# Three constant products instead of one on TensorE between the steps on wo's two halves

## The chip, the cores and the metric

The kernel runs on one core of a Trainium2 chip (trn2). The metric is the device time of one execution in microseconds; of several executions the median is given. Engine names are those of the profile: PE is TensorE, PEld its weight loads, DVE VectorE, ACT ScalarE, POOL GpSimd, SP SyncE; a q behind a name means the engine's sequencer or its DMA issues.

## The reference

One decode step for two batch rows, a gated mix of attention over the last 4096 cached positions and a dense layer with Mish:

```
B, Sq, D = 2, 1, 512;  Hq, Hkv, Sk, Dh = 32, 8, 32768, 128;  F = 1792
W = min(4096, max(256, Sk // 4))
def _A_ref(x, k_cache, v_cache, wq, wo):
    q = (x @ wq).reshape(B, Sq, Hq, Dh).transpose(0, 2, 1, 3)
    k, v = the last W positions of k_cache, v_cache, each head repeated Hq // Hkv times
    p = softmax(einsum("bhqd,bhkd->bhqk", q, k) * Dh ** -0.5)
    return einsum("bhqk,bhkd->bhqd", p, v).reshape(B, Sq, Hq * Dh) @ wo
def _B_ref(x, w1, b1, w2):
    h = x @ w1 + b1
    return (h * tanh(softplus(h))) @ w2
g = sigmoid((x * gate_w).sum(-1, keepdims=True))
return g * _A_ref(...) + (1 - g) * _B_ref(...)
```

All arrays are float32. What has to be read is about 91 MB: the eight heads' K and V (4 MB each), wq and wo (8 MB each), w1 and w2 (3.5 MB each).

## The kernel before

**Chunks and steps.** The big arrays come in as chunks of 128 partitions x 8192 float32 (4 MB) that are loaded in turn into two buffers, `buf_b` and `buf_a` (`load`, L349 to L359). A chunk is sixteen slots of 512 columns. A *step* on a buffer (`slots`, L369) multiplies each slot with 32 weight columns on TensorE; the product of slot s goes to rows 32·(s mod 4) to 32·(s mod 4)+31 of one PSUM bank, so that four slots in a row use four different column strips of the array. The eleven steps on `buf_b` are wq's first half, K of heads 0 to 7, w1 and wo's second half; the eleven on `buf_a` are wq's second half, V of heads 0 to 7, wo's first half and the larger part of w2. Between them stand "turns" (L409 to L417): four transposes of `turn` into `t_b`, a small product with `ones`, and one *constant product*.

**The constant product** (`idle_work`, L392) multiplies the 128x128 identity by four copies of itself into the bank `b_idle`, which nothing reads. It has no data to wait for and is there to occupy TensorE.

**The loop.** TensorE's program is a loop of three bodies, and a register `n` counts the steps on `buf_a`: it starts at `FULL - steps_a` = 6 (L399) and is raised by one behind each step on `buf_a` (L420). After each step L421 sets `spin` to `n & 16`, that is 0 up to V of head 7 and 16 after wo's first half. As long as `n` is at most 16, L422 goes to the body "spin" (L402): one constant product, `spin` raised by one (L404), and back to the constant product while `spin` is under `SPINS` = 5 (L405). So there are five constant products behind each of the steps before wo, and one behind the step on wo's first half, where `spin` is 17 after one pass. Then "step_b" runs on `buf_b`, which at that point is wo's second half; with `n` = 16 it goes on to "step_a" without a turn (L408), and that step is w2's.

**The end of the program**, in order, with the numbers that the prediction follows:

- step on wo's first half (`buf_a`, bank `g_a`). When it is done, SP issues the five last loads (L363 to L366): w2's blocks 0 to 7 and 8 to 10 into slots 5 to 12 and 13 to 15 of `buf_a` (semaphores `s4`, `s12`), and three single blocks into `rest` (`sr`). ACT copies `g_a` into `sums` (L316), and POOL sets up the weights of w2's step in `la` (L317, L318);
- the constant product (L393 in the body "spin");
- step on wo's second half (`buf_b`, bank `g_b`), which waits at slot 0 for the landing of its chunk (`sb`);
- step on w2 (`buf_a`, bank `g_a`): it waits at slot 0 for `la` (`sa`), at slot 5 for `s4`, at slot 13 for `s12` (L419; the waits are L372). Slots 0 to 4 have zero weights and wait for no transfer;
- "products" (L423, `finish`, L334): the first two blocks in `rest`, each behind its landing, then `sums` times a fold matrix, then the last block in `rest`, all four into `b_fin`. `sums` becomes ready by two additions on DVE: `g_b` when wo's second half is done (L321) and `g_a` when the step on w2 is done (L322);
- DVE copies `b_fin` into `res` (L344) and SP stores it (L367).

Loads go out from SP in program order, each into its buffer as soon as the step that used the buffer before is done.

## Time and profile before

| | us |
|---|---|
| median of 3 runs (219.75 to 219.83) | 219.81 |
| the profiled execution's own time | 219.8 |
| its span, first to last instruction | 217.8 |
| PE busy / DVE / ACT / POOL | 158.2 / 26.8 / 16.6 / 14.2 |
| constant products (61, each two records of 128x512) | 58.3 |
| read from HBM, mean rate | 91.24 MB, 419 GB/s |
| mean granted TensorE clock | 0.961 |

The page gives the busy time of each engine and a picture of the span in 40 slices; a PEclk digit under 9 there is a slice in which TensorE's clock was granted only in part. The view of windows gives, for chosen stretches of the span, each engine's busy time, the granted clock and the rate of the DMAs. The timeline lists instructions in order, merged, with the idle time before them in brackets. Each float32 product on TensorE leaves two matmul records.

### The profile page before, as it was taken

What the parts mean: (1) busy time and instruction counts of PE and PEld (TensorE: products, weight loads), DVE (VectorE), ACT (ScalarE), POOL (GpSimd) and SP (SyncE); (2) the same over time, 40 slices, a digit from 0 to 9 for tenths busy, and PEclk for the clock granted to TensorE, in tenths of its full rate; (3) what the DMA queues carried; (4) which work ended last, traced back from release to release, by engine and by line L of the source; (5) the groups of instructions that cost most, each with busy time, mean ns of one, the idle gap of its engine ahead of it and who ended that gap; (6) DMA issues with size and microseconds to landing.
All of it is one profiled execution on the core that took longest, in us unless ns stands there. A gap on an engine that the chain in (4) does not pass through costs nothing. (4 is left out here: it accounts for less than half of the span.)

```text
span 217.8 us, 2358 instructions
## 1 busy us (share of the span) xinstructions
PE 158.2 (73%) x948; PEld 58.0 (27%) x948; DVE 26.8 (12%) x49; ACT 16.6 (8%) x39; POOL 14.2 (7%) x44
## 2 busy tenths in 40 slices
PE   0048976897577649965983976599399689989495
PEld 0012222332122223322321322132123233343132
DVE  0000001030102102110310301030103103062011
ACT  0021001200200110020002002000200120020100
POOL 4040101000100100010010001000100030003000
PEclk9999999999999988997999999799969999999979
DMA  8999999999999999999999999999999999999992
GB/s 290 392 476 391 475 391 475 391 475 391 475 391 475 391 475 391 475 391 475 391 469 397 469 397 469 397 469 391 469 397 469 397 445 421 469 397 463 391 407 97
DMA packets 3985, 91.30 MB, mean 419 GB/s; under 512 B 576, under 2 KB 656, under 8 KB 1168
## 3 DMA queue, kind: packets, MB, share of 16 engines
q1 hardware_dynamic: 3840, 91.27, 97.6%
q10 hardware_dynamic: 144, 0.01, 0.1%
q8 instruction: 1, 0.02, 0.0%
HBM read 91.24 MB, written 0.04 MB: 419 GB/s over the span
## 5 line engine op out<-in xcount | busy, mean ns | idle before, releaser
L373 PE MATMUL bank<-buf_b,zeros 128*32 128x512 f32 x352 | 44.3, 648 | 23.7 <-PEq L372 23.7
L373 PE MATMUL bank<-buf_a,zeros 128*32 128x512 f32 x352 | 46.1, 671 | 17.9 <-PEq L372 17.9
L393 PE MATMUL bank<-ident 128*128 128x512 f32 x122 | 58.3, 608 | 0.0
L393 PEld LDWEIGHTS bank<-ident 128*128 128x128 f32 x122 | 21.2, 190 | 25.6 <-issue 25.6
L373 PEld LDWEIGHTS bank<-buf_b,zeros 128*32 128x32 f32 x352 | 12.9, 117 | 53.2 <-issue 53.2
L373 PEld LDWEIGHTS bank<-buf_a,zeros 128*32 128x32 f32 x352 | 13.8, 121 | 49.2 <-issue 49.2
L412 PE MATMUL bank<-ident,turn 128*128 128x128 f32 x60 | 9.4, 280 | 15.6 <-PEq L410 15.6
L209 ACT ACTIVATE turn<-bank,mx 128x512 f32<-128x512 f32 x8 | 5.5, 687 | 132.5 <-DVE mx L207 132.5
L230 DVE TENSOR_TENSOR om<-bank,pick 128x512 f32<-128x512 f32 x8 | 5.5, 692 | 73.6 <-PE bank L373 73.6
L412 PEld LDWEIGHTS bank<-ident,turn 128*128 128x128 f32 x60 | 6.3, 140 | 28.3 <-issue 28.3
L207 DVE TENSOR_REDUCE mx<-bank 128x1 f32<-128x512 f32 x8 | 5.5, 692 | 63.5 <-PE bank L373 63.5
L202 POOL COPY zeros<-zeros 128x512 f32<-128x512 f32 x8 | 4.9, 616 | 125.7 <-PE bank L373 125.7
L233 DVE TENSOR_REDUCE od<-om 128x128 f32<-128x512 f32 x8 | 8.3, 1036 | 0.3
L211 ACT COPY zeros<-bank 128x512 f32<-128x512 f32 x8 | 4.7, 586 | 7.9 <-PE bank L413 7.9
L413 PE MATMUL bank<-zeros,ones 128*128 128x66 f32 x30 | 5.0, 249 | 0.0
L413 PEld LDWEIGHTS bank<-zeros,ones 128*128 128x128 f32 x30 | 4.5, 191 | 0.0
L182 ACT ACT_TABLE_LOAD x1 | 1.3, 1283 | 14.6 <-POOL ident L165 14.6
L158 POOL MEMSET zeros<- 128x2490 f32 x1 | 2.2, 2173 | 0.3 <-POOLq L478 0.3
L226 POOL TENSOR_TENSOR ms<-ms,top 8x64 f32<-8x64 f32 x2 | 0.6, 309 | 23.9 <-DVE top L224 23.8
L321 DVE TENSOR_TENSOR sums<-sums,bank 128x512 f32<-128x512 f32 x1 | 0.7, 687 | 11.5 <-PE bank L373 11.5
L175 DVE TENSOR_REDUCE zeros<-xg 128x2 f32<-128x8 f32 x1 | 0.2, 163 | 13.9 <-POOL xg L162 13.9
L273 ACT COPY turn<-od 128x512 f32<-128x512 f32 x1 | 0.6, 617 | 14.6 <-PE bank L413 14.6
(68 smaller groups left out, 22.6 us busy)
## 6 DMA issues: line engine op xcount, KB each, us to landing
buf_b<-in_k SPq DMA_DIRECT2D x8, 4096.0 KB, 15.5
buf_a<-in_v SPq DMA_DIRECT2D x8, 4096.0 KB, 14.9
buf_b<-in_wq SPq DMA_DIRECT2D x1, 4096.0 KB, 12.3
buf_a<-in_wq SPq DMA_DIRECT2D x1, 4096.0 KB, 21.5
buf_a<-in_wo SPq DMA_DIRECT2D x1, 4096.0 KB, 14.4
buf_b<-in_wo SPq DMA_DIRECT2D x1, 4096.0 KB, 15.5
buf_b<-in_w SPq DMA_DIRECT2D x1, 3584.0 KB, 14.3
buf_a<-in_w SPq DMA_DIRECT2D x1, 2048.0 KB, 8.8
```

The lines of the kernel that those rows point to most:

```text
L158: zero_ok = t = pool.add(lambda: G.memset(zeros, 0.0))
L182: act.add(lambda: S.activation(turn, g_b, AF.Copy, scale=SCALE), xs_ok, id_ok, at("B q0"), sem=st)
L202: pool.add(lambda kv=kv: G.tensor_copy(lb.rearrange("p (m j q) -> p m j q", m=BN, j=NJ), qz[:, kv, : BN * Q].rearrange("p (m q) -> p m q", ...
L207: mx_ok = dve.add(lambda kv=kv: V.tensor_reduce(mx[:, kv : kv + 1], g_b, axis=AX.X, op=ALU.max, negate=True), before_b)
L209: act.add(lambda kv=kv: S.activation(turn, g_b, AF.Exp, bias=mx[:, kv : kv + 1], accum_out=ls[:, kv : kv + 1]), mx_ok, sem=st)
L211: act.add(lambda: S.copy(la, t_b), at(f"T p{kv}"), sem=sa, by=1 if kv else 2)
L230: t = dve.add(lambda: V.tensor_tensor(om, g_a.rearrange("p (m d) -> p m d", m=BN), pick[:, :, None].to_broadcast([P, BN, DH]), op=ALU.mult ...
L233: dve.add(lambda kv=kv: V.tensor_reduce(od[:, kv], om.rearrange("p m d -> p d m"), axis=AX.X, op=ALU.add), t, sem=sa)
L373: ins = T.matmul(bank[Q * (s % NJ) : Q * (s % NJ) + Q, :], weights[:, s * Q : (s + 1) * Q], buf[:, s * D : (s + 1) * D], start=(s < NJ), s ...
L393: T.matmul(b_idle, ident, ident[:, None, :].to_broadcast([P, NT, P]), start=True, stop=True)
L412: T.transpose(t_b[:, c * P : (c + 1) * P], turn[:, c * P : (c + 1) * P], ident)
L413: T.matmul(b_s[:, : HKV * BH + B], ones, kx, start=True, stop=True).then_inc(pe.sem, 1)
```

## The change

The loop counter of the constant products goes up in strides of eight to a limit of 40:

```diff
-SPINS = 5
+SPINS = 40
 FULL = 16
+STRIDE = 8
...
             part("spin")
             idle_work()
-            eng.reg_add(spin, spin, 1)
+            eng.reg_add(spin, spin, STRIDE)
             eng.br_lt(spin, SPINS, "spin", "step_b")
```

From `spin` = 0 the counter passes 8, 16, 24, 32, 40: five constant products, as before. From `spin` = 16, behind the step on wo's first half, it passes 24, 32, 40: three constant products instead of one. No other engine's program changes, and the list of TensorE's instructions stays the same; only the number of passes through one loop differs. All lines of the kernel from the new constant on stand one line lower.

## The prediction

> **What bounds the kernel now.** I read the picture of the span first. The rows are PE's busy tenths, the granted clock, the DMA share and the rate, in 40 slices of 5.44 us:

> ```profile
> PE   0048976897577649965983976599399689989495
> PEclk9999999999999988997999999799969999999979
> DMA  8999999999999999999999999999999999999992
> GB/s 290 392 476 391 475 391 475 391 475 391 475 391 475 391 475 391 475 391 475 391 469 397 469 397 469 397 469 391 469 397 469 397 445 421 469 397 463 391 407 97
> ```

> The transfers fill the span up to the last slice, so a change on TensorE counts only where TensorE is late against the transfers, and that is the end. Six digits of PEclk stand under 9. At the first five of them (slices 15, 16, 19, 26 and 30) the transfers run on regardless; the last, the 7 in the last slice but one, lies just ahead of the end. The chain of work that ended last says the same (start, length, what):

> ```profile
> 205.49 0.04 issue
> 205.54 8.80 PE bank L373 x64
> ...
> 214.43 0.70 DVE sums L322
> 215.13 0.04 issue
> 215.18 0.69 PE bank L334 x16
> ...
> 215.89 0.29 DVE res L344
> ```

> From 205.54 us on nothing but TensorE's two last steps and a short tail sets the end. The timeline of PE there (start, length, line, operands, records, idle before), with one earlier run of five constant products:

> ```profile
> 181.26 4.56 PE L393 MATMUL bank<-ident 128*128 128x512 f32 x10
> ...
> 197.85 3.64 PE L373 MATMUL bank<-buf_a,zeros 128*32 128x512 f32 x32 [0.45 <-PEq L372]
> 201.42 1.13 PE L393 MATMUL bank<-ident 128*128 128x512 f32 x2
> 205.54 5.34 PE L373 MATMUL bank<-buf_b,zeros 128*32 128x512 f32 x32 [2.99 <-PEq L372]
> 210.66 3.64 PE L373 MATMUL bank<-buf_a,zeros 128*32 128x512 f32 x32
> 214.10 0.65 PE L334 MATMUL bank<-rest,zeros 128*32 128x128 f32 x16
> 215.18 0.43 PE L334 MATMUL bank<-sums,zeros 128*32 128x128 f32 x8 [0.43 <-DVE sums L322]
> 215.42 0.40 PE L334 MATMUL bank<-rest,zeros 128*32 128x128 f32 x8
> ```

> Two steps with the same 32 records stand side by side: the one on w2 goes from 210.66 to 214.10, 3.44 us; the one on wo's second half goes from 205.54 to 210.66, 5.12 us, 1.68 us more. Ahead of the slow one lie the single constant product and 2.99 us of idle.

> **Why that step is slow.** The view of windows, cut into stretches of 3.41 us whose edges I laid on the point where records turn slow (206.58). Columns: stretch, its length, busy us of PE, PEld, DVE, ACT, POOL with counts, granted clock, DMA share, GB/s:

> ```profile
> 97.35:100.76 3.41, 0.80 (x9) 0.28 (x12) 0.00 (x0) 0.00 (x0) 0.00 (x0) 1.00 0.94 404
> 100.76:104.18 3.42, 3.42 (x24) 1.09 (x20) 0.00 (x0) 0.00 (x0) 0.00 (x0) 0.50 0.93 402
> ...
> 117.83:121.24 3.41, 1.60 (x16) 0.65 (x20) 0.00 (x0) 0.00 (x0) 0.00 (x0) 1.00 0.89 384
> 121.24:124.66 3.42, 3.42 (x24) 1.21 (x17) 1.29 (x2) 0.00 (x0) 0.00 (x0) 1.00 1.00 431
> ...
> 134.90:138.31 3.41, 1.45 (x8) 0.62 (x6) 0.00 (x0) 0.59 (x1) 0.00 (x0) 1.00 0.91 394
> 138.31:141.72 3.41, 2.75 (x16) 0.92 (x20) 0.00 (x0) 0.00 (x0) 0.00 (x0) 0.50 0.94 404
> ...
> 199.75:203.16 3.41, 2.80 (x21) 0.61 (x10) 0.00 (x0) 0.59 (x1) 0.72 (x4) 1.00 1.04 452
> 203.16:206.58 3.42, 1.04 (x12) 0.50 (x16) 0.00 (x0) 0.00 (x0) 0.00 (x0) 1.00 0.94 402
> 206.58:209.99 3.41, 3.41 (x23) 1.08 (x16) 0.00 (x0) 0.00 (x0) 0.00 (x0) 0.50 0.97 412
> 209.99:213.40 3.41, 3.41 (x36) 1.26 (x32) 0.69 (x1) 0.00 (x0) 0.00 (x0) 1.00 1.00 399
> ```

> Read each row's PE busy together with the clock of the next row. After 0.80, 1.45 and 1.04 us of work the next stretch has half the clock; after 1.60 and 2.80 us it has all of it; a busy stretch at half clock brings the full one back. So on this grid the clock is halved for 3.41 us when the stretch before was busy for less than something between 1.45 us (42%) and 1.60 us (47%). The cost here is half of 3.41, 1.71 us, against the 1.68 us by which the step is too long: one halved stretch explains it.

> [...]

> **The change part by part.** It adds two passes of one loop at one place. All other loops keep their counts: from 0 the counter reaches 40 after five passes, from 16 after three.

> *The two products.* Five take 4.56 us and one takes 1.13, so one more is (4.56 - 1.13) / 4 = 0.86 us, and three take 1.13 + 1.72 = 2.85 us: they end at 201.42 + 2.85 = 204.27 instead of 202.55. The next step starts at 205.54, so 1.27 us of idle are left and the added 1.72 us cost nothing as long as wo's second half lands no earlier than now. That start is set by a landing, as the rows of the waits in the steps (L372; each row is one wait, "first and last start" is its time) and of the loads show:

> ```profile
> L372 PEldq EVENT_SEMAPHORE  x1: 51/51/51, 205.4 to 205.4; - x1
> L372 PEldq EVENT_SEMAPHORE  x1: 51/51/51, 210.3 to 210.3; - x1
> L372 PEldq EVENT_SEMAPHORE  x1: 51/51/51, 212.2 to 212.2; - x1
> buf_b<-in_wo SPq DMA_DIRECT2D x1, 4096.0 KB, 15.5
> buf_a<-in_w SPq DMA_DIRECT2D x1, 2048.0 KB, 8.8
> buf_a<-in_w SPq DMA_DIRECT2D x1, 768.0 KB, 10.3
> rest<-in_w SPq DMA_DIRECT2D x1, 256.0 KB, 10.7
> ...
> 189.91 0.33 SPq L350 DMA_DIRECT2D buf_b<-in_wo  x1
> 201.54 0.80 SPq L350 DMA_DIRECT2D buf_a<-in_w  x2
> 202.39 1.38 SPq L350 DMA_DIRECT2D rest<-in_w  x3
> ```

> wo's second half lands at 189.91 + 15.5 = 205.4, where its wait ends; the first product follows 0.1 us later. Nothing else is queued behind the two products but that step: `b_idle` has no reader, and SP, ACT and POOL are released by the step before.

> *The clock.* In the stretch from 203.16 to 206.58 PE now works 204.27 - 203.16 = 1.11 us longer, 2.15 us in all (63%), above the 1.60 us after which the clock stayed. So 206.58 to 209.99 keeps the full clock, and the step on wo's second half takes 3.44 us: 205.54 to 208.98, 1.68 us earlier than before.

> *What is late next.* Not all of the 1.68 us reaches the end, for the step on w2 waits at slot 5 and slot 13 for its own transfers. The first one lands at 201.54 + 8.8 = 210.34, the second, issued at about 201.9, at 201.9 + 10.3 = 212.2, just where the wait rows above stand; before, TensorE's sequencer had run ahead to these waits and the array was later than both. Now the array is ahead. Its pace at full clock shows in the weight loads of that step, four column strips at a time:

> ```profile
> 210.66 0.16 PEld L373 LDWEIGHTS bank<-buf_a,zeros 128*32 128x32 f32 x4 [0.27 <-issue]
> 211.09 0.16 PEld L373 LDWEIGHTS bank<-buf_a,zeros 128*32 128x32 f32 x4 [0.27 <-issue]
> ```

> Four records, one of each of four slots, per 0.43 us, two such groups per four slots: 0.86 us. Slots 0 to 3 run from 208.98 to 209.84; slot 4 follows alone; slots 5 to 7 start at 210.34 + 0.1 = 210.44 (the 0.1 as between 205.4 and 205.54) and end at 211.30; slots 8 to 11 end at 212.16; slots 13 to 15 start at 212.2 + 0.1 = 212.3 and end at 213.16. Before, the step ended at 214.10, so it ends 0.94 us earlier.

> *The tail.* The addition on DVE (214.43 before, 0.33 behind the step's end) starts at 213.49, takes its 0.70, and 0.05 later, at 214.24 instead of 215.18, the fold product follows; the last product runs at 214.48 instead of 215.42. The last block lands 10.7 us after its issue, the third of the row at 202.39 with 1.38 us for three, so at about 203.3 + 10.7 = 214.0, and 0.1 later its product could run: 214.1, in time for 214.48 with 0.4 us to spare. Copy and store keep their lengths.

> **The sum.** Added work 0; clock -1.68; given back by the waits on w2 +0.74; -0.94 us in all. The profiled execution took 219.80 us (span 217.8, 2.0 around it), which is the median of 219.81 to 0.01: 219.80 - 0.94 = 218.86, or **218.9 us**.

> *Bounds.* No row shows a step of this kind resumed in the middle of a group of four. If slot 4 fills a group of its own before slots 5 to 7 may start, it holds the array until 210.70, slots 5 to 7 end at 211.56, 8 to 11 at 212.42, and 12 to 15, whose wait is over by then, at 213.28: a gain of 0.82. If slot 12 too fills a group alone, the step ends at 214.14 and the gain is about -0.04. If the strips instead share the array by slots (0.215 each), slots 13 to 15 end at 212.95 and the last block's landing takes over: 214.1 instead of 215.42, a gain of 1.3 and the most that the transfers allow. I take 0.94, since the records run in step strip by strip and a strip that starts late should only delay itself.

> **The rivals.**

> *The clock falls all the same* (219.8, no change). If only a stretch without any work counted, the fall would have another cause and the products would not touch it. [...] Against it stand all the halved stretches shown, each behind one with 0.80 to 1.45 us of work. A variant: the edges of the stretches lie elsewhere in other executions. The idle of 2.99 us halves the clock if one stretch holds more than about 1.81 us of it (3.41 - 1.60), which fails only where an edge splits it nearly evenly, in some 20% of the positions; the 1.27 us left after the change can reach 1.81 at no position. So the forecast does not hang on the grid; only a run of before might be shorter by chance, and 219.75 to 219.83 shows none. 7%.

> *The gain is hidden by transfers* (219.8). It would be gone if w2's blocks landed 0.9 us later. For it: they already take back 0.74. Against it: they are issued behind wo's first half, before the added products, and the rate is 399 to 452 GB/s in the stretches where PE works 2.80 to 3.41 us, and 384 to 404 where it works 0.80 to 1.60, so more work on PE doesn't slow them. That the loop doesn't run three passes belongs here too. 4%.

> *The low stretch moves onto the last step* (slower). If the clock were judged on a later stretch, so that the waits at slots 5 and 13 count as quiet and the half clock sets in with slot 5 at 210.44, then 3.41 us at half bring 1.71 us of the three groups' 2.58 by 213.85, and the other 0.87 end the step at 214.72 instead of 214.10: 0.62 us more than before, 220.4 us. It decides only if PE is busy for less than 1.60 us in the 3.41 us ahead of that, where I find the step on wo until 208.98 and slots 0 to 4 behind it. With another unforeseen loss, 5%.

> **How the numbers follow.** The forecast has 84%, the rivals 7, 4 and 5. The range reaches from the most that the transfers allow, 219.8 - 1.3 = 218.5, up to a gain of 0.5, 219.3, which covers the slot groups' first bound and about half of the gap to no gain; rivals and the outer bound lie outside with some 17%. About 0.2% (0.44 us) is what a measurement of this kernel can tell from no change: faster by more 84%, within it 11%, slower 5%.

> **What would show it.** Right: 126 records of the constant product instead of 122, three in a row ending near 204.3; no halved clock behind 203 us; the step on wo's second half 3.4 to 3.5 us long from an unchanged 205.5; idle in the w2 step ahead of 210.4; the fold product near 214.3. Wrong: a clock of 0.50 anywhere between 203 and 214; landings of w2 away from 210.3 and 212.2; a w2 step that ends at 214.1 although its predecessor ended at 209.0 (the slot groups' bound).

## The result, and the profile after

The changed kernel took 219.13 us in the median of 8 runs (218.85 to 219.51); the kernel before took 219.82 us in 8 runs beside it (219.70 to 220.15). The ratio is 0.9968, with a 95% interval of 0.9957 to 0.9979: 0.3% faster, 0.69 us of medians. The profiled execution took 218.91 us, 0.89 us less than the one of before, with a span of 216.9 us.

The picture of the span of the changed kernel, granted clock alone (40 slices of 5.42 us):

```profile
PEclk9999999999999999997999999999969999999999
```

The 7 in the last slice but one is gone. The low digits of before at slices 15, 16 and 26 are gone too, though the change touches nothing there; the experiments below show how the places of the halved stretches move from execution to execution. The timeline of PE at the end, beside the one in the prediction:

```profile
181.35 4.56 PE L394 MATMUL bank<-ident 128*128 128x512 f32 x10
...
201.51 2.84 PE L394 MATMUL bank<-ident 128*128 128x512 f32 x6
205.62 3.64 PE L374 MATMUL bank<-buf_b,zeros 128*32 128x512 f32 x32 [1.26 <-PEq L373]
209.05 4.39 PE L374 MATMUL bank<-buf_a,zeros 128*32 128x512 f32 x32
213.02 0.94 PE L335 MATMUL bank<-rest,zeros 128*32 128x128 f32 x16
214.30 0.42 PE L335 MATMUL bank<-sums,zeros 128*32 128x128 f32 x8 [0.34 <-DVE sums L323]
214.54 0.40 PE L335 MATMUL bank<-rest,zeros 128*32 128x128 f32 x8
```

Six records instead of two behind wo's first half; the idle time ahead of wo's second half is 1.26 us instead of 2.99. That step goes from 205.62 to 209.05, 3.43 us instead of 5.12. The next one is drawn out, 4.39 us instead of 3.64. The whole timeline stands 0.08 to 0.09 us later than before; it does so already at 181.35 (before: 181.26), far ahead of the change.

The chain of work that ended last:

```profile
205.62 7.84 PE bank L374 x64
...
213.56 0.70 DVE sums L323
214.25 0.04 issue
214.30 0.69 PE bank L335 x16
...
215.01 0.29 DVE res L345
```

It has the same links as before; TensorE's piece is 7.84 us long instead of 8.80.

The windows of the same trace, with edges where its own clock changes (203.03 and every 3.41 us from there; columns as in the prediction):

```profile
199.62:203.03 3.41, 3.41 (x24) 1.27 (x17) 0.00 (x0) 0.59 (x1) 0.88 (x4) 1.00 1.07 461
203.03:206.45 3.42, 2.16 (x12) 0.60 (x14) 0.00 (x0) 0.00 (x0) 0.00 (x0) 1.00 0.92 393
206.45:209.86 3.41, 3.41 (x36) 1.21 (x29) 0.47 (x1) 0.00 (x0) 0.00 (x0) 1.00 0.94 400
```

Where the stretch before held 1.04 us of work, this one holds 2.16, and the next has the full clock.

The waits inside the steps and the weight loads of w2's step show what took part of the gain back:

```profile
L373 PEldq EVENT_SEMAPHORE  x1: 51/51/51, 205.5 to 205.5; - x1
L373 PEldq EVENT_SEMAPHORE  x1: 51/51/51, 210.4 to 210.4; - x1
L373 PEldq EVENT_SEMAPHORE  x1: 51/51/51, 212.3 to 212.3; - x1
```

```profile
209.05 0.16 PEld L374 LDWEIGHTS bank<-buf_a,zeros 128*32 128x32 f32 x4 [0.27 <-issue]
...
209.48 0.11 PEld L374 LDWEIGHTS bank<-buf_a,zeros 128*32 128x32 f32 x1 [0.27 <-issue]
209.91 0.11 PEld L374 LDWEIGHTS bank<-buf_a,zeros 128*32 128x32 f32 x1 [0.32 <-issue]
210.46 1.28 PEld L374 LDWEIGHTS bank<-buf_a,zeros 128*32 128x32 f32 x16 [0.44 <-issue]
212.35 0.18 PEld L374 LDWEIGHTS bank<-buf_a,zeros 128*32 128x32 f32 x6 [0.61 <-issue]
```

The landings are where they were. The groups of four weight loads thin out to single ones (slot 4 alone) up to the wait at 210.4; a second gap lies ahead of 212.35, behind the wait at 212.3.

### The profile page after: what moved, and what is told of

Read it like the earlier page. It is cut to its first block, busy times and chain, and to the rows that moved or that the text cites. A ratio compares the mean times of both kernels' runs of the same rounds, so it can differ in the third digit from the quotient of the medians.

```text
span 216.9 us, 2370 instructions
## 1 busy us (share of the span) xinstructions
PE 156.5 (72%) x952; PEld 58.1 (27%) x952; DVE 26.8 (12%) x49; ACT 16.6 (8%) x39; POOL 14.2 (7%) x44
## 5 line engine op out<-in xcount | busy, mean ns | idle before, releaser
L374 PE MATMUL bank<-buf_b,zeros 128*32 128x512 f32 x352 | 42.8, 628 | 24.2 <-PEq L373 24.2
L394 PE MATMUL bank<-ident 128*128 128x512 f32 x126 | 60.0, 607 | 0.0
L374 PE MATMUL bank<-buf_a,zeros 128*32 128x512 f32 x352 | 44.2, 637 | 18.3 <-PEq L373 18.3
L394 PEld LDWEIGHTS bank<-ident 128*128 128x128 f32 x126 | 22.0, 190 | 26.6 <-issue 26.6
L374 PEld LDWEIGHTS bank<-buf_b,zeros 128*32 128x32 f32 x352 | 12.4, 114 | 52.5 <-issue 52.5
L322 DVE TENSOR_TENSOR sums<-sums,bank 128x512 f32<-128x512 f32 x1 | 0.7, 689 | 9.8 <-PE bank L374 9.8
## 6 DMA issues: line engine op xcount, KB each, us to landing
buf_b<-in_k SPq DMA_DIRECT2D x8, 4096.0 KB, 15.5
buf_a<-in_v SPq DMA_DIRECT2D x8, 4096.0 KB, 15.5
buf_b<-in_wq SPq DMA_DIRECT2D x1, 4096.0 KB, 12.3
buf_a<-in_wq SPq DMA_DIRECT2D x1, 4096.0 KB, 21.6
buf_a<-in_wo SPq DMA_DIRECT2D x1, 4096.0 KB, 14.4
buf_b<-in_wo SPq DMA_DIRECT2D x1, 4096.0 KB, 15.5
buf_a<-in_w SPq DMA_DIRECT2D x1, 2048.0 KB, 8.7
```

Source lines behind the costliest of these rows:

```text
L374: ins = T.matmul(bank[Q * (s % NJ) : Q * (s % NJ) + Q, :], weights[:, s * Q : (s + 1) * Q], buf[:, s * D : (s + 1) * D], start=(s < NJ), s ...
L394: T.matmul(b_idle, ident, ident[:, None, :].to_broadcast([P, NT, P]), start=True, stop=True)
```

## The experiments

Kernels that are compared ran on one chip, between runs of the kernel before; on the three chips used there are 90 such runs. What each timed run lists beside its time is the span and the mean granted clock. One stretch of 3.41 us at half clock in a span of 217.8 lowers the mean by 0.5 · 3.41 / 217.8 = 0.0078, so that (1 - 0.961) / 0.0078 = 5 stretches, as the trace of before shows them. So the mean clock of a run tells about how many of its stretches were halved, if not where. The kernel before by that count:

| mean granted clock | halved stretches | runs | time, us (median) |
|---|---|---|---|
| 0.968, 0.969 | 4 | 20 | 218.66 to 220.20 (218.92) |
| 0.961 | 5 | 41 | 219.42 to 221.71 (219.86) |
| 0.953 | 6 | 17 | 220.76 to 221.89 (221.18) |
| 0.976 and more | 2 or 3 | 12 | 218.72 to 220.08 (219.76) |

The kernel before does not have one time but three: 16 of the 90 runs are at most 219.0 us, 44 lie between 219.6 and 220.4, and 20 above 220.4; ten lie between the first two groups. The count alone does not give the time: the runs with two or three halved stretches belong partly to the first group and mostly to the second, since what matters is whether a halved stretch falls on the last steps, as the one at 206.58 does in the trace of before (5.12 us for the step instead of 3.44). Nor is all of the scatter clock: in 11 of the 90 runs the time is 2.4 to 2.6 us longer than the span, instead of 2.0, and what happens outside the span there no trace shows. The changed kernel, 29 runs in all: 218.79 to 219.73, median 219.04, one of them above 219.6.

**Two products, five products.** A limit of 30 in strides of 7 gives two passes behind wo's first half and five elsewhere; 100 in strides of 20 gives five in both places. The edit for two:

```diff
-SPINS = 40
-STRIDE = 8
+SPINS = 30
+STRIDE = 7
```

> Two constant products behind wo's first half instead of three (limit 30, stride 7; the five elsewhere stay). Theory (a stretch of 3.41 us with less than 1.45 to 1.60 us of TensorE work halves the clock of the next one): the products end near 203.4, so about 2.1 us of idle are left. On the grid of the two traces so far the stretch before 206.5 would hold 1.3 us of work, the clock is halved, and the time is that of before, 219.8. If the grid lies elsewhere in every execution, about half of the positions halve the clock: runs near 219.8 and runs near 219.1, with nothing to do between them. Rival (every added product helps in proportion, no threshold): 219.4 to 219.5 in all runs.

Measured: 219.41 us median, and no run near it. Six of twelve lie at 218.79 to 219.12, six at 219.69 to 219.96. The profiled one (219.90) is of the upper group; its windows and timeline:

```profile
202.48:205.90 3.42, 1.29 (x7) 0.38 (x9) 0.00 (x0) 0.00 (x0) 0.31 (x2) 1.00 0.89 378
205.90:209.31 3.41, 3.41 (x20) 1.08 (x16) 0.00 (x0) 0.00 (x0) 0.00 (x0) 0.50 1.03 442
```

```profile
201.53 1.98 PE L394 MATMUL bank<-ident 128*128 128x512 f32 x4
205.64 5.34 PE L374 MATMUL bank<-buf_b,zeros 128*32 128x512 f32 x32 [2.13 <-PEq L373]
```

With 1.29 us of work in its stretch (38%) the clock falls, and the second product has bought nothing in this run; in the other half of the runs it has bought everything. A limit on the work of a stretch fits that, and a gain per product, which would have put all runs at 219.4 to 219.5, doesn't. And the edges lie elsewhere than in the trace of before: 205.90 here, 206.58 there, 206.45 in the changed kernel, 204.76 in the one below, all against a landing at 205.4 to 205.6. So in these four traces the grid of stretches does not stand at one place after the start of the span.

> Five constant products behind wo's first half (limit 100, stride 20). Theory: no idle is left; the products reach 206.0, the step on wo's second half starts 0.2 us late, and the wait for w2's first blocks at 210.4 takes these 0.2 us up again: the time of three products, 219.1 within 0.1, clock full up to the end. Rival (the cover ends with three, more work on TensorE is late at the end): 0.2 to 1.7 us above the changed kernel, 219.4 to 220.8.

Measured: 219.02 us median (218.67 to 219.89). The timeline of the profiled run (219.02):

```profile
201.49 4.56 PE L394 MATMUL bank<-ident 128*128 128x512 f32 x10
205.97 3.64 PE L374 MATMUL bank<-buf_b,zeros 128*32 128x512 f32 x32
209.43 4.10 PE L374 MATMUL bank<-buf_a,zeros 128*32 128x512 f32 x32
213.11 0.93 PE L335 MATMUL bank<-rest,zeros 128*32 128x128 f32 x16
```

The step starts 0.35 us later than with three and w2's step is shorter by nearly as much, since it has 0.3 us less to wait. Five products cost what three do in the median: the theory holds. Five of the twelve runs lie above 219.3, which it does not explain; for two of them, 219.31 and 219.33, the spans are only 216.8 and 216.9 us, as in the short runs, so that some 0.5 us lie outside the span.

**w2's load cut short.** Only one block goes into slots 5 to 12 and one into 13 to 15; the products are all there and work on what the buffer held. One kernel with one constant product, one with three:

```diff
-    parts = [(a3[:, PART + CUTS[x] : PART + CUTS[x + 1]], sem, at("A wo")) ...
+    parts = [(a3[:, PART + CUTS[x] : PART + CUTS[x] + 1], sem, at("A wo")) ...
...
-        load(flat(dst), w2[f0 * D * P : f1 * D * P]...
+        load(flat(dst), w2[f0 * D * P : (f0 + 1) * D * P]...
```

> One constant product as before, and of w2's blocks 0 to 7 and 8 to 10 only one each is loaded (blocks 1 to 7, 9 and 10 are left out of the load, the products stay), so that w2's step never waits for a landing. Theory: the clock is halved as before, TensorE's two steps set the end as before, 219.8. Rival (the transfers of w2 set the end already before): some us less, 217 to 219.

> Three constant products as in the changed kernel, with the same short load of w2 as in the kernel with one product (blocks 1 to 7, 9 and 10 are left out of the load, the products stay). Theory (the clock gives 1.68 us and the waits for w2's landings take 0.74 of it back): the whole 1.68 us show, 218.1, that is 1.7 below the kernel with one product and the same load. If the spread of the changed kernel's runs (218.85 to 219.51) comes from w2's landings, it is gone here. Rival (the clock gives only the 0.7 to 0.9 us that were measured): 218.9 to 219.1.

Measured: 219.85 us with one product (12 runs: four at 218.02 to 218.32, seven at 219.70 to 220.22, one at 221.18) and 218.09 with three (6 runs, 217.95 to 218.24). The difference of the medians is 1.76 us, near the clock's 1.68 and not the 0.7 to 0.9 of the full kernel. It is a difference between mixtures: the four short runs with one product are as fast as those with three, as if the grid had spared the step there, and the seven in the middle lie 1.6 to 2.1 us above 218.09. With three, w2's step takes its plain length:

```profile
201.54 2.84 PE L394 MATMUL bank<-ident 128*128 128x512 f32 x6
205.67 3.64 PE L374 MATMUL bank<-buf_b,zeros 128*32 128x512 f32 x32 [1.29 <-PEq L373]
209.10 3.64 PE L374 MATMUL bank<-buf_a,zeros 128*32 128x512 f32 x32
212.54 0.65 PE L335 MATMUL bank<-rest,zeros 128*32 128x128 f32 x16
213.62 0.43 PE L335 MATMUL bank<-sums,zeros 128*32 128x128 f32 x8 [0.43 <-DVE sums L323]
```

It ends at 212.54, and the fold product stands at 213.62 instead of the changed kernel's 214.30. So w2's landings are what took the missing part back. The spread shrinks with them: 0.29 us between the shortest and the longest of six runs, against 0.94 for the changed kernel's 29. The profiled run of the kernel with one product is the one of 221.18 and shows what six halved stretches are:

```profile
201.35:204.76 3.41, 1.38 (x6) 0.30 (x2) 0.00 (x0) 0.58 (x1) 0.43 (x2) 1.00 0.79 342
204.76:208.18 3.42, 2.46 (x12) 0.69 (x16) 0.00 (x0) 0.00 (x0) 0.00 (x0) 0.50 0.97 371
208.18:211.59 3.41, 3.41 (x20) 0.92 (x16) 0.00 (x0) 0.00 (x0) 0.00 (x0) 0.50 0.02 6
```

The clock falls at 204.76, and the stretch that follows, idle for its first 0.95 us, does not bring it back: 2.46 us of work (72%) at half clock are too little. So the step on wo's second half takes 6.34 us there (205.72 to 212.06). In the trace of before 2.75 us (80%) were enough:

```profile
138.31:141.72 3.41, 2.75 (x16) 0.92 (x20) 0.00 (x0) 0.00 (x0) 0.00 (x0) 0.50 0.94 404
141.72:145.14 3.42, 3.42 (x26) 1.09 (x17) 1.10 (x2) 0.00 (x0) 0.00 (x0) 1.00 1.02 441
```

How much work keeps the full clock is less sharp in these figures than the rows in the prediction make it look. In the trace of the changed kernel 1.37 us were enough:

```profile
117.70:121.11 3.41, 1.37 (x16) 0.58 (x20) 0.00 (x0) 0.00 (x0) 0.00 (x0) 1.00 1.00 432
121.11:124.53 3.42, 3.42 (x27) 1.23 (x20) 1.06 (x2) 0.00 (x0) 0.00 (x0) 1.00 1.02 441
```

In the trace of the next kernel 1.49 us were not:

```profile
134.89:138.31 3.42, 1.49 (x8) 0.66 (x6) 0.00 (x0) 0.58 (x1) 0.00 (x0) 1.00 0.96 412
138.31:141.72 3.41, 2.72 (x16) 0.86 (x20) 0.00 (x0) 0.00 (x0) 0.00 (x0) 0.50 0.89 384
```

Over all thirteen traces, each cut along its own edges from its first record of the clock on (at 18.84 us in the trace of before), 1.49 us (44%) is the most work after which the clock fell, and 1.34 us (39%, in the trace with five products) the least after which it stayed. The two overlap, perhaps because a row's busy time is not exact: in the trace of before the records of w2's step make 3.64 us, and the next product starts 3.44 us after the first of them. The 1.04 and 1.29 us ahead of halved last steps lie below both figures, and the 2.16 us of the changed kernel above both. A second limit for the way back up is not shown either: 2.46 us at half clock are 1.23 us of work at the full clock, and 2.75 are 1.38, so that one limit on work, near 1.3 to 1.5 us, would fit both ways.

**Products of a quarter of the array.** One product as before (limit 5, stride 1), then two of the same length that load 32 of 128 weight columns, in a body of their own ahead of wo's second half:

```diff
-            eng.br_lt(n, FULL + 1, "spin", "products")
+            eng.br_lt(n, FULL, "spin", "last")
+            part("last")
+            eng.br_eq(n, FULL, "extra", "products")
+            part("extra")
+            idle_work()
+            for _ in range(2):
+                T.matmul(b_idle[:Q, :], ident[:, :Q], ident[:, None, :].to_broadcast([P, NT, P]), start=True, stop=True)
+            eng.br("step_b")
```

> One constant product as before, then two products of the same length in time (512 columns) but with 32 instead of 128 weight columns, so that they use a quarter of the array. Theory (what counts for the clock is the time in which TensorE works): as the changed kernel, median near 219.0, no run near 219.8 or 221. Rival (what counts is how much of the array works): the two products count for 0.4 us instead of 1.7, the stretch stays under 43% in most positions of the grid, and the median is near 219.8 as before.

Measured: 219.06 us median (218.84 to 219.52, none near 219.8 or 221). Timeline and windows of the profiled run:

```profile
201.46 1.13 PE L394 MATMUL bank<-ident 128*128 128x512 f32 x2
202.51 1.90 PE L429 MATMUL bank<-ident 128*32 128x512 f32 x4
205.56 3.64 PE L374 MATMUL bank<-buf_b,zeros 128*32 128x512 f32 x32 [1.14 <-PEq L373]
208.99 4.84 PE L374 MATMUL bank<-buf_a,zeros 128*32 128x512 f32 x32
```

```profile
203.16:206.57 3.41, 2.27 (x15) 0.60 (x17) 0.00 (x0) 0.00 (x0) 0.00 (x0) 1.00 0.94 394
206.57:209.98 3.41, 3.41 (x37) 1.17 (x27) 0.65 (x1) 0.00 (x0) 0.00 (x0) 1.00 0.97 413
```

Of the 2.27 us, 1.25 (203.16 to 204.41) are narrow products. At a quarter they would leave 0.3 + 1.0 = 1.3 us, where the clock fell ahead of the last steps in the kernels above (1.29 and 1.38); it stays. This trace alone would be close, since 1.34 us were once enough; the twelve runs are not. At a quarter, one product and two narrow ones would be less work than the two products above, of which half the runs lay near 219.8; here none does. What counted in these runs is the time in which TensorE works, 2.27 us in the row above, not how many of the array's columns do.

This run, at 219.52, also shows one thing that the upper end of the changed kernel's runs can be; none of the traces is of a long run of the changed kernel itself. Its waits for w2's landings:

```profile
L373 PEldq EVENT_SEMAPHORE  x1: 51/51/51, 210.8 to 210.8; - x1
L373 PEldq EVENT_SEMAPHORE  x1: 51/51/51, 212.7 to 212.7; - x1
```

Both are 0.4 us later than in the changed kernel while wo's second half landed as usual, and the end is later by as much. In the packets of this trace the first packet of w2's load took 1.41 us on one of the 16 DMA engines and 1.11 on another, against 0.61 to 0.67 for all others of its size in that load, and one engine's packets of that load ended 0.37 us behind all others. That the slow first packets are the reason is likely, not shown. The clock is full (1.00) in both rows above, up to 209.98.

**The changed kernel again, w2 in a buffer of its own, and another cut.** With a buffer of its own w2's load need not wait for the step on wo's first half; it is issued at 190.4 instead of 201.5. The step on w2 becomes a body of its own (`step_w2`) that reads slots 5 to 15 there. The other edit moves one block from the group of three to the single ones behind it:

```diff
+    w2b = sb("w2b", SLOTS, D)
...
-    parts = [(a3[:, PART + CUTS[x] : PART + CUTS[x + 1]], sem, at("A wo")) ...
+    parts = [(w2b[:, PART + CUTS[x] : PART + CUTS[x + 1]], sem, None) ...
```

```diff
-CUTS = (0, 8, 11, 12, 13, 14)
+CUTS = (0, 8, 10, 11, 12, 13, 14)
```

> The changed kernel once more, beside kernels of the same call, for the spread of its runs and a second trace. Theory: no position of the 3.41 us grid leaves a stretch below 43% of work, so no run near 219.8 or 221 of the two upper groups of before; median 218.9 to 219.1. What stays open is a tail of single runs up to 219.5: if it comes from w2's landings, it is seen here and gone in the kernel with w2's own buffer; if it comes from the clock, the trace of such a run shows a halved stretch between 203 and 214.

> Three constant products; w2's eleven first blocks go to a buffer of their own, so that their loads are issued right behind wo's second half near 190.5 and no longer wait for the step on wo's first half. Theory 1 (the loads were already queued in time, back to back): landings at 210.3 and 212.2 as before, median as the changed kernel, and its tail of slower runs stays. Theory 2 (in some runs the issue near 201.5 is too late and w2's landings slip): median 218.8 to 218.9, all runs within 0.3 us.

> Three constant products; w2 is cut after block 10 instead of 11, so that slots 14 and 15 wait for two blocks and four single blocks follow. Theory (the end hangs on the landing that the w2 step waits for last, then 0.86 us of slots, 0.33, the addition of 0.70 and the fold): that landing comes 0.6 us earlier, near 211.6, the fold near 213.65, and now the last block, landed at 214.1, starts its product at 214.2 instead of 214.54: 0.3 us less than the changed kernel, 218.6 to 218.7. Rival (the last single block bound the end already): no change.

Measured, on one chip: again 218.96 us (9 runs, 218.86 to 219.21); own buffer 218.89 (218.67 to 219.18, and one run of 221.90 with six halved stretches); the cut 218.99 (six runs at 218.59 to 218.87, six at 219.11 to 220.12). In the cut's trace (218.66) the fold product stands at 214.05, 0.25 us ahead of the changed kernel's and not at 213.65 as expected: though the landing that the step waits for last comes 0.6 us earlier, slots 14 and 15, whose last records start at 212.57 and 212.61, seem to follow slots 10 and 11 on their strips, which started with the landing before. Of its six upper runs the longest has a halved stretch more than the others; in the other five the time is 2.4 to 2.6 us longer than the span instead of 2.0, so that about half a microsecond of each lies outside the span. Why is open. On another chip, with both edits together as the third:

> The changed kernel, as the partner of the two kernels with w2's own buffer on the same chip. Its runs lay between 218.85 and 219.51 in the first measurement and between 218.86 and 219.21 in the second. Theory 2 (a first packet of w2's load that is slow on one or two DMA engines when the loads are issued near 201.5 moves w2's landings by up to 0.8 us): median 218.95 to 219.1, some runs at 219.2 to 219.6 with no more halved stretches than the short ones.

> w2's blocks in a buffer of their own once more, loads issued near 190.5. Theory 2: again a median of 218.85 to 218.9, at least 0.1 us under the partner, and nothing above 219.2 but a run with extra halved stretches, like the one of 221.9 with six. Rival (the early issue changes nothing and 218.89 against 218.96 was chance): median within 0.05 us of the partner and a tail as long.

> w2's own buffer and the cut after block 10 together. Theory 2 with the landing order as measured for the cut alone (fold at 214.05, the last product at 214.29, best runs 218.6): 218.6 to 218.7 in nearly all runs, the upper half of the cut alone (219.1 to 220.1) gone. Rival (the upper half has another cause, in the end that now hangs on the last block): median near 219.0 with the same split.

Measured: again 219.08 us (218.79 to 219.73); own buffer 219.05 (218.88 to 219.44); both edits 218.73 (218.51 to 219.07), in the ratio to before 0.9956 (0.9936 to 0.9977). Both edits together are the best version here, 0.35 us below the changed kernel on the same chip, every run at or under 219.07. The own buffer alone is not shown to help: 0.07 and 0.03 us below its partner, where at least 0.1 was expected, and the tail was there on the second chip, with four runs above 219.2. None of its three traces (both edits included) has a slow first packet of w2's load, and six of the eight with the full load issued near 201.5 have one to three; that the early issue is the reason remains likely and not settled. Nor does a slow first packet make a run long by itself: the changed kernel's run of 219.05 has one of 1.17 us, and its fold product follows the start of wo's second half 8.68 us later, as in the run of 218.91. What else makes the tail is open.

## Why the prediction was right, point by point

- *The two products are hidden.* Right: they end at 204.35, the step starts 0.1 us behind its landing, with 1.26 us of idle left (forecast 1.27).
- *The clock.* Right: 2.16 us of work in the stretch (forecast 2.15), full clock in the next, the step 3.43 us long (3.44). The limit of 1.45 to 1.60 us was that of one trace; over all of them it lies between 1.34 and 1.49 us and is not sharp, and 2.15 is clear of it by either reading. The rival that only an empty stretch halves the clock fell with the kernel of two products, where 1.29 us of work were not enough. The traces show stretches of 3.41 us, with edges at 206.58, 206.45, 205.90 and 204.76 in four of them (the trace with quarter products, 206.57, happens to have the grid of before).
- *What is late next.* Right: waits at 210.4 and 212.3; the addition on DVE starts at 213.56, so the step ended 0.33 us ahead of that, at 213.23, with the 0.08 us of the later start in it (forecast 213.16). The strips behave as assumed: slot 4 ran ahead alone and delayed nothing but its own strip, so the bounds of -0.04 and 0.82 did not come up. Without w2's landings about the whole 1.68 us show (1.76 between the medians of the two kernels with the short load; 218.1 was expected for the one with three products, 218.09 measured).
- *The tail.* Right: fold at 214.30 (forecast 214.24, and 0.08 later start), last product at 214.54 (214.48).
- *The sum.* 218.9 forecast, 218.91 in the profiled execution, 219.13 in the median of that measurement and 219.04 over 29 runs. That the profiled execution meets the forecast to the last tenth is luck: it is the second shortest of its eight runs. The 0.1 to 0.2 us by which the medians are longer probably belong to the step that took w2's landings as unchanged: with the short load, where nothing waits for them, time and forecast agree and the spread is small, and in one trace the landings are 0.4 us late. What was covered by 0.9 us of late TensorE work before would then stand at the end. A part of the longer runs stays unexplained.
- *The grid.* That the idle of before leaves the clock alone in some 20% of the positions agrees with the 90 runs (16 of 90 at 219.0 or less); that the runs known then had none was chance. Not seen at all: the second halved stretch, when the edge lies such that the idle reaches into the first one. Of the 20 runs of before above 220.4, 17 have six halved stretches by their mean clock. None of the changed kernel's 29 runs is that long, so the change removes these too; but one run of the kernel with w2's own buffer, which has the same three products, took 221.90 with six halved stretches, and what happened in it no trace shows.

## What to carry to other kernels

Look up what the granted clock does in the last wait of a kernel and ahead of the steps that set the end: half a clock cost nothing here where transfers bound the time (runs of the changed kernel with two and with four halved stretches took 218.91 and 218.85 us), and where TensorE does it cost 1.7 us for one halved stretch and 2.9 us on the same step in the one trace with two. The dose is to be worked out from the idle that is left: filler must bring a stretch of 3.41 us in every position above the limit (1.49 us of work were too little here), since the grid moved from run to run (edges at 206.58, 206.45, 205.90 and 204.76 in four traces); one product too few left half of the runs near 219.8, two too many cost nothing in the median. And read the gain against the next landing: here 1.68 us became 0.9.
